# Converting weight pieces in pairs, fetching the first piece first, and a lag of one block in batch 0

## The chip, the cores and the metric

The kernel runs on one core of a Trainium2 chip. The metric is device time in microseconds, the median of several executions. The core has five engines with instruction queues of their own: PE (matmuls), DVE and ACT (elementwise), POOL, and SP, which here issues every DMA. Each engine takes its instructions in the order in which they were built, and waits on semaphores for the others.

## The reference, cut to what matters

For 8 batches of 8 heads, 576 rows of 64 columns, 32 packed rows per head attend to the whole sequence, and then the sequence attends to the 32 packed results. The attention output is reshaped to 4608 tokens of 512 columns and goes through a two-layer network with a Mish activation. The weights are of type float64, as numpy makes them.

```python
p_packed = sm_attn(p, k, v)                      # softmax(scale * p k^T) v
out = sm_attn(q, p_packed, p_packed)
x = attn_out.transpose(0, 2, 1, 3).reshape(B * S, H * D)
h = x @ w_in                                     # 512 x 2048
g = h * np.tanh(sp)                              # sp = log1p(exp(h)), Mish
return g @ w_out                                 # 2048 x 512
```

## The kernel before

**Stages.** An opening computes the attention of batch 0, written out step by step. After it a loop runs over `t`, one step for each batch `b` and block `f` of 128 of the 2048 hidden columns (16 blocks per batch, `NF`). In each step PE does the up product of block `f` in two halves of 288 tokens (`Group.up`, L618 to L634) and the down product of an earlier block in four parts of 128 tokens (`down`, L660; part c is "down c"). ACT applies Mish to each up half and writes `g`. The earlier block is `LAG` = 2 steps back. The attention of batch b + 1 is a generator (`Later.attention`) that is advanced some two or three times in a step, so that it lies between these products.

**Up without the values matrix.** The up product uses `packed_w` (L570): for each chunk of 512 hidden columns (4 blocks) the packed values of the batch are multiplied into w_in once, 16 matmuls into two PSUM tiles `ps_w`; ACT writes the high part `wp_hi`, DVE the low part `wp_lo`. In batch 0, chunk c + 1 is packed in the last block of chunk c (f = 3, 7, 11), between down 2 and the second up half. `ps_w` shares its two PSUM buffers (`ps_a`) with the scores and values of the attention.

**Weights.** w_in and w_out arrive as 32 pieces of 512 KB of 64-bit words (`Weight`: chunk c, row block m; `WeightOut`: block f). A piece is fetched by one DMA into one of `STB` = 10 stage buffers (`fetch`); ACT makes two passes over its words, one into the destination and one into a buffer `wround`, of which there are 3 (`words`); DVE joins them in four steps, each of which works on the result of the one before (`join`, L550 to L559). The last step frees `wround`; the third is the last that reads the stage buffer. In batch 0 the down product uses w_out as converted; later batches use a high and a low half, made by `split_wo` from step 14 on.

**What sets the order.** In the opening PE and SP stand in the order of the code, and DVE and ACT are put in order by a scheduler when the program is built. From the end of the opening to step 16 all of them stand in the order of the code, except that a few of the first of these rows are placed among the last of the opening. Behind step 16 the scheduler orders SP, DVE and ACT again. `upto` (L731) and `join_next` (L739) decide which piece is fetched, gets its words and is joined: after the four pieces of chunk 0, w_in and w_out pieces alternate, and each step joins two, one after up 0 and one after up 1, with words one piece ahead. A stage buffer is refilled when the piece ten places ahead of it has been joined.

Of the kernel before, what the change touches and what calls it, by code (L numbers as in the profile page):

```python
# [16 lines left out]
LAG = 2  # L17
# [3 lines left out]
STB = 10  # L21
# [13 lines left out]
def body(  # L35
# [22 lines left out]
    NF = DF // P  # L58
# [52 lines left out]
    def load_heads(src, b, g, tag):  # L111
        ts = []
        for h0 in (4 * g, 4 * g + 2):
            t = early.tile([R, 2, NI, 2 * D], F32, name=tag, tag="kvq", bufs=KVB)
            nc.sync.dma_start(
                out=t, in_=src[b, h0:h0 + 2].rearrange("h (p i x) d -> p h i (x d)", i=NI, x=2)
            )
            ts.append(t)
        return ts
# [411 lines left out]
    class Weight:  # L531
# [18 lines left out]
        def join(self):  # L550
            dst, bits = self.dst, self.dst.bitcast(I32)
            nc.vector.tensor_scalar(
                out=dst, in0=dst, scalar1=F64_HIGH, scalar2=-F64_HIGH, op0=ALU.min, op1=ALU.max
            )
            nc.vector.tensor_scalar(out=bits, in0=bits, scalar1=3, scalar2=None, op0=ALU.logical_shift_left)
            nc.vector.scalar_tensor_tensor(
                out=bits, in0=self.high, scalar=-0x80000000, in1=bits, op0=ALU.bitwise_and, op1=ALU.bitwise_or
            )
            nc.vector.tensor_tensor(out=bits, in0=bits, in1=self.r, op=ALU.add)  # L559

    class WeightOut(Weight):
# [146 lines left out]
    def advance(gen):  # L708
        flush()
        next(gen, None)  # L710
# [11 lines left out]
    n_groups = B * NF  # L722

    pieces = [Weight(0, m) for m in range(4)]
    for f in range(NF):
        if f < 12:
            pieces.append(Weight(1 + f // 4, f % 4))
        pieces.append(WeightOut(f))
    pieces_done = {"fetch": 0, "words": 0, "join": 0}

    def upto(step, n):  # L731
        while pieces_done[step] < min(n, len(pieces)):
            k = pieces_done[step]
            getattr(pieces[k], step)()
            pieces_done[step] += 1
            if step == "join":
                upto("fetch", k + 1 + STB)

    def join_next(n):  # L739
        for _ in range(n):  # L740
            k = pieces_done["join"]
            upto("words", k + 1)
            upto("join", k + 1)
            upto("words", k + 2)

    with tc.manual_schedule(engines={mybir.EngineType.PE}):
        for _ in range(8):
# [1 line left out]
        first = batches[0]  # L749
        by_hand = ExitStack()  # L750
        by_hand.enter_context(tc.manual_schedule(engines={mybir.EngineType.SP}))
        first.k_t = [load_heads(k, 0, 0, "k_t")]
        first.load_p()
        upto("fetch", 1)
        first.k_t.append(load_heads(k, 0, 1, "k_t"))
        first.v_t = [load_heads(v, 0, 0, "v_t")]
        first.q_t = [load_heads(q, 0, 0, "q_t")]
        upto("fetch", 2)
        first.v_t.append(load_heads(v, 0, 1, "v_t"))
        first.q_t.append(load_heads(q, 0, 1, "q_t"))  # L760
        upto("fetch", STB)
        first.start(ps_a)
        score = [first.score_now(g) for g in range(2)]
        for _ in range(3):
            next(score[0])
        upto("words", 1)
        next(score[0], None)
        upto("join", 1)
        next(score[1])
        next(score[1])  # L770
        together(first.turn_weights(0, ps_acc, ("ACT", "ACT")))
        next(score[1])
        next(score[1], None)
# [2 lines left out]
        together(first.turn_values(0, ps_a))  # L776
        together(first.turn_weights(1, ps_acc, ("ACT", "ACT")))
        together(first.match(0, ps_acc))
        upto("words", 2)
        first.peak(slice(0, 1))  # L780
        first.rise(slice(0, 1))
        upto("join", 2)
        together(first.values(1, ps_a))
        together(first.turn(1, ps_acc, ("ACT", "ACT", "ACT")))
        together(first.turn_values(1, ps_a))
        together(first.match(1, ps_acc))
        upto("words", 3)
        first.peak(slice(1, 2))
        first.rise(slice(1, 2))
        first.weigh(slice(0, 1))  # L790
        upto("words", 4)
        upto("join", 4)
        wps = {(0, 0): packed_w(0, 0)}
        first.weigh(slice(1, 2))
        by_hand.enter_context(tc.manual_schedule(engines={mybir.EngineType.DVE, mybir.EngineType.Activation}))
        upto("words", 5)
        groups = []
        gen = iter(())
        g_rest = None
        for t in range(n_groups + LAG):  # L800
            b, f = divmod(t, NF)
            grp = None
            if t < n_groups:
                if f == 0:
                    if b % 2 == 0:
                        g_rest = ([], [])
                if f == (1 if b else ATT0) and b + 1 < B:
                    gen = batches[b + 1].attention()
                if t == LOAD0:
                    opening.close()  # L810
                    kv.append(ctx.enter_context(tc.tile_pool(name="kv", bufs=2, side="left", reuse_waits="tile")))
                    for _ in range(KQB):
                        load_next()
                grp = Group(b, f, wps[b, f // 4], g_rest)
                grp.tiles()
            groups.append(grp)
            dn = groups[t - LAG] if t >= LAG else None
            joins = 2 if t < 14 else 0
            if t == NF:
                by_hand.close()  # L820
            if t == SPLIT0:
                stage.close()
                late.append(ctx.enter_context(tc.tile_pool(name="late", bufs=1, side="right", reuse_waits="tile")))
            if 0 <= t - SPLIT0 < NF:
                split_wo(t - SPLIT0)
            if dn:
                down(dn, 0)
            if grp:
                grp.up(0)
            chunk = b == 0 and f % 4 == 3 and f < NF - 1  # L830
            if not chunk:
                advance(gen)
            join_next(joins - joins // 2)
            if dn:
                down(dn, 1)
                down(dn, 2)
            if chunk:
                flush()
                wps[0, f // 4 + 1] = packed_w(0, f // 4 + 1)
            else:  # L840
                advance(gen)
            if grp:
                grp.up(1)
                grp.halves()
            join_next(joins // 2)
            if dn and dn.b % 2 == 1 and dn.f % 4 == 2:
                rest["g"] = split(dn.g_rest[0][dn.f // 4], dn.g_rest[1][dn.f // 4])
            if dn:
                down(dn, 3)
            if grp and f % 4 == 2 and (b or f == NF - 2):  # L850
                nb, nch = divmod(b * (NF // 4) + f // 4 + 1, NF // 4)
                if nb < B:
                    flush()
                    if nb > b:
                        finish(gen)
                    wps[nb, nch] = packed_w(nb, nch)
            elif b == 0 and not chunk:
                advance(gen)
            if dn and dn.b % 2 == 1 and dn.f % 4 == 3:
                flush()  # L860
                down_rest(dn)
# [26 lines left out]
```

## Time and profile before

| | us |
|---|---|
| median of 3 runs (778.96 to 779.28) | 779.27 |
| the profiled execution, whole | 777.98 |
| its span, first to last instruction | 776.2 |
| PE busy | 740.1 (95%) |
| DVE busy | 440.8 (57%) |
| ACT busy | 297.3 (38%) |

In the page's 40 slices of 19.4 us, PE stands at 6, 7, 7, 7, 8, 9 and 6 tenths in the first seven and at 9 after that. All 32 weight pieces arrive in the first six slices, in which the mean busy share of the DMA engines is 8 to 9 tenths or more. Times below are in microseconds from the start of the span. A row of the order of time gives start, duration, engine, line, operation, output and inputs, count, and in brackets the idle time before it and what ended it. Durations of neighbours on one engine can overlap, so what a row costs its engine is read from start to start. A matmul in 32 bits shows as two records, so four records of `acc` are two downs.

### The profile page before, as it was taken

The numbers are of one execution on the slowest core, as the hardware profiler recorded it, in microseconds if no ns is written. First come the engines' busy times: TensorE is split into PE (matmuls) and PEld (weight loads), VectorE is DVE, ScalarE is ACT, GpSimd is POOL, SyncE is SP. The second block draws the span as 40 slices with busy tenths as digits, with TensorE's granted clock in tenths as the row PEclk, the third lists the DMA queues.
The fourth block names the chain that finished last, engine by engine and source line by source line (L and its number), as shares of the span: only waits on it lengthen the run. The fifth ranks groups of instructions, "written<-read, shape, count | busy, mean of one in ns | idle before, by whom it ended". The sixth has DMA issues, their size and how long they took to land.

```text
span 776.2 us, 12461 instructions
## 1 busy us (share of the span) xinstructions
PE 740.1 (95%) x5044; PEld 565.9 (73%) x5044; DVE 440.8 (57%) x788; ACT 297.3 (38%) x685; POOL 0.7 (0%) x6
## 2 busy tenths in 40 slices
PE   6777896999999999999999999999999999999997
PEld 4453553568788787878788787878788787888886
DVE  4888898964663636554663636554673636432332
ACT  3563654824242334224342244224242244322221
POOL 0000000000000000000000000000000000000000
PEclk9998998999999999999999999999999999999999
DMA  9999980032510534032510434032400200010002
GB/s 248 338 194 275 223 197 0 1 86 41 98 23 1 119 58 84 1 85 38 103 21 1 113 61 86 1 85 32 92 1 1 69 2 1 1 55 1 0 1 69
DMA packets 184825, 56.39 MB, mean 73 GB/s; under 512 B 173760, under 2 KB 176064, under 8 KB 184768
## 3 DMA queue, kind: packets, MB, share of 16 engines
q1 hardware_dynamic: 184768, 55.59, 30.8%
q8 instruction: 40, 0.66, 0.4%
q14 instruction: 17, 0.14, 0.1%
HBM read 46.14 MB, written 9.44 MB: 72 GB/s over the span
## 4 chain that ended last, share of the span: by engine, by line
PE 85%; DVE 6%; DMA 5%; SPq 2%; issue 1%; ACT 0%; DVEq 0%
PE ps_h L627 25%; PE acc L646 15%; PE acc L648 13%; PE acc L647 13%; PE ps_w L577 5%; PE acc L666 3%; DMA w_st<-in_moe_w_in_dram 3%; PE ps_s L396 2%; PE ps_rest L647 2%; PE ps_rest L648 2%; PE ps_rest L646 2%; SPq L341 2%; DMA w_st<-in_moe_w_out_dram 1%; PE ps_pp L451 1%; DVE xT L386 1%
## 5 line engine op out<-in xcount | busy, mean ns | idle before, releaser
L630 ACT ACTIVATE g<-ps_h 128x288 f32<-128x288 f32 (+1 forms) x256 | 97.6, 384 | 322.7 <-PE ps_h L627 293.3
L646 PE MATMUL acc<-wo_hi,g_hi 128*128 128x512 f32 x448 | 183.9, 410 | 0.0
L648 PE MATMUL acc<-wo_hi,g_lo 128*128 128x512 f32 x448 | 176.4, 394 | 0.0
L647 PE MATMUL acc<-wo_lo,g_hi 128*128 128x512 f32 x448 | 176.2, 393 | 0.0
L627 PE MATMUL ps_h<-aT_hi,wp_hi 128*128 128x288 f32 x512 | 165.2, 323 | 4.7 <-ACT aT_hi L297 4.7
L627 PE MATMUL ps_h<-aT_lo,wp_hi 128*128 128x288 f32 x512 | 152.8, 298 | 1.4 <-DVE aT_lo L300 1.4
L627 PE MATMUL ps_h<-aT_hi,wp_lo 128*128 128x288 f32 x512 | 152.0, 297 | 0.0
L641 DVE CAST g_hi<-g 128x512 fp32r<-128x512 f32 x112 | 47.6, 425 | 169.8 <-ACT g L630 169.6
L627 PEld LDWEIGHTS ps_h<-aT_hi,wp_hi 128*128 128x128 f32 x512 | 97.7, 191 | 27.1 <-issue 7.5
L646 PEld LDWEIGHTS acc<-wo_hi,g_hi 128*128 128x128 f32 x448 | 84.0, 187 | 43.4 <-issue 28.4
L627 PEld LDWEIGHTS ps_h<-aT_lo,wp_hi 128*128 128x128 f32 x512 | 97.8, 191 | 17.0 <-issue 6.0
L648 PEld LDWEIGHTS acc<-wo_hi,g_lo 128*128 128x128 f32 x448 | 84.0, 188 | 19.7
L627 PEld LDWEIGHTS ps_h<-aT_hi,wp_lo 128*128 128x128 f32 x512 | 97.7, 191 | 0.0
L647 PEld LDWEIGHTS acc<-wo_lo,g_hi 128*128 128x128 f32 x448 | 84.3, 188 | 9.0 <-issue 0.2
L642 DVE TENSOR_TENSOR g_lo<-g,g_hi 128x512 fp32r<-128x512 f32 x112 | 77.3, 690 | 6.3 <-DVE g_hi L641 0.5
L666 PE MATMUL acc<-wo,g 128*128 128x512 f32 x128 | 63.2, 609 | 0.0
L577 PE MATMUL ps_w<-wi,ppT 64*32 64x512 f32 x512 | 41.8, 634 | 15.1 <-DVE wi L559 7.1
L589 DVE TENSOR_TENSOR wp_lo<-ps_w,wp_hi 128x512 fp32r<-128x512 f32 x64 | 41.3, 683 | 24.8 <-ACT wp_hi L588 24.8
L588 ACT CAST wp_hi<-ps_w 128x512 fp32r<-128x512 f32 x64 | 34.4, 590 | 50.4 <-PE ps_w L577 50.4
L666 PEld LDWEIGHTS acc<-wo,g 128*128 128x128 f32 x128 | 22.7, 196 | 15.4 <-issue 13.8
L577 PEld LDWEIGHTS ps_w<-wi,ppT 64*32 64x32 f32 x512 | 7.6, 108 | 31.4 <-issue 17.1
L632 ACT ACTIVATE g_rest<-ps_h 128x64 f32<-128x64 f32 x128 | 28.1, 220 | 0.0
(107 smaller groups left out, 688.8 us busy)
## 6 DMA issues: line engine op xcount, KB each, us to landing
w_st<-in_moe_w_in_dram SPq DMA_DIRECT2D x16, 512.0 KB, 7.8
w_st<-in_moe_w_out_dram SPq DMA_DIRECT2D x16, 512.0 KB, 5.7
k_n<-in_k_dram SPq DMA_DIRECT2D x56, 144.0 KB, 3.1
q_n<-in_q_dram SPq DMA_DIRECT2D x56, 144.0 KB, 3.2
v_n<-in_v_dram SPq DMA_DIRECT2D x56, 128.0 KB, 2.8
out_dram<-o SPq DMA_DIRECT2D x28, 256.0 KB, 2.0
k_t<-in_k_dram SPq DMA_DIRECT2D x4, 288.0 KB, 5.0
v_t<-in_v_dram SPq DMA_DIRECT2D x4, 288.0 KB, 8.6
```

Source lines behind the costliest of these rows:

```text
L577: nc.tensor.matmul(out=ps[g][h * NP:(h + 1) * NP, :], lhsT=ppTb[row:row + D, g, h * NP:(h + 1) * NP], rhs=wi[c][g][row:row + D, h // 2, :] ...
L588: nc.scalar.copy(out=hi, in_=ps[g])
L589: nc.vector.tensor_tensor(out=lo, in0=ps[g], in1=hi.bitcast(F32), op=ALU.subtract)
L627: nc.tensor.matmul(out=ps, lhsT=w[:, fs], rhs=a[:, g, cs], start=(n == 0), stop=(n == 5))
L630: nc.scalar.activation(out=self.act[:, hf * HALF:hf * HALF + m], in_=ps[:, :m], func=AF.Mish)
L632: nc.scalar.activation(out=self.g_rest[self.b % 2][self.f // 4][:, self.f % 4, :], in_=ps[:, m:], func=AF.Mish)
L641: nc.vector.tensor_copy(out=hi, in_=self.act)
L642: nc.vector.tensor_tensor(out=lo, in0=self.act, in1=hi.bitcast(F32), op=ALU.subtract)
L646: nc.tensor.matmul(out=acc, lhsT=hi[:, cs], rhs=wh, start=start, stop=False)
L647: nc.tensor.matmul(out=acc, lhsT=hi[:, cs], rhs=wl, start=False, stop=False)
L648: nc.tensor.matmul(out=acc, lhsT=lo[:, cs], rhs=wh, start=False, stop=stop)
L666: nc.tensor.matmul(out=accs[c], lhsT=grp.act[:, cs], rhs=wo[f], start=f == 0, stop=f == NF - 1)
```

## The change

The diff, without the functions that it replaces:

```diff
             nc.vector.tensor_scalar(
                 out=dst, in0=dst, scalar1=F64_HIGH, scalar2=-F64_HIGH, op0=ALU.min, op1=ALU.max
             )
+            yield
             nc.vector.tensor_scalar(out=bits, in0=bits, scalar1=3, scalar2=None, op0=ALU.logical_shift_left)
+            yield
...
     pieces = [Weight(0, m) for m in range(4)]
-    for f in range(NF):
-        if f < 12:
-            pieces.append(Weight(1 + f // 4, f % 4))
-        pieces.append(WeightOut(f))
...
+    pieces += [WeightOut(0), Weight(1, 0), Weight(1, 1), WeightOut(1), Weight(1, 2), Weight(1, 3)]
+    pieces += [WeightOut(2), WeightOut(3)]
+    for c in (2, 3):
+        for e in range(2):
+            pieces += [Weight(c, 2 * e), Weight(c, 2 * e + 1), WeightOut(4 * c - 4 + 2 * e), WeightOut(4 * c - 3 + 2 * e)]
+    pieces += [WeightOut(i) for i in range(12, NF)]
...
+    def join(n):
+        words(n)
+        together(*[x.join() for x in pieces[done["join"]:n]])
+        done["join"] = max(done["join"], min(n, len(pieces)))
+        fetch(n + STB)
...
+        fetch(1)
         first.k_t = [load_heads(k, 0, 0, "k_t")]
         first.load_p()
-        upto("fetch", 1)
         first.k_t.append(load_heads(k, 0, 1, "k_t"))
+        fetch(2)
...
-            dn = groups[t - LAG] if t >= LAG else None
-            joins = 2 if t < 14 else 0
+            lag = 1 if t <= NF else LAG
+            dn = groups[t - lag] if t >= lag and t != NF + 1 else None
...
-            join_next(joins - joins // 2)
+            if t <= 12:
+                words(2 * t + 8)
+                join(2 * t + 8)
+                words(2 * t + 10)
             if dn:
                 down(dn, 1)
-                down(dn, 2)
             if chunk:
                 flush()
                 wps[0, f // 4 + 1] = packed_w(0, f // 4 + 1)
-            else:
+            if dn:
+                down(dn, 2)
+            if not chunk:
                 advance(gen)
...
-            join_next(joins // 2)
```

In words: `join` is now a generator that stops after each step, and two pieces are joined with their steps in turn (first piece step 1, second piece step 1, first piece step 2, and so on). In the loop one pair is joined per step, after up 0, and the words of the next pair follow it. The pieces are in another order: each chunk of w_in is now joined two steps or more before it is packed, and w_out blocks come one step before their down product. In the opening `join(2)`, `join(4)` and `join(6)` stand where single pieces stood, and the first weight DMA is the first DMA of all. In batch 0 the down product lags one step instead of two (step 17 has none, so that later batches lag two again), and in the last block of a chunk the packed weights come before down 2 instead of behind it.

Three places show what the change does to the queues. First, ACT in the opening, behind the exponentials of the first scores' second half: `wi0`, `wi1` are w_in of chunk 0 and 1, `wo32` is w_out, `qT` and `a1T` are copies that the attention of batch 0 needs. Before:

```order
L547 ACTIVATE wi0_1_92<-w_st_145 128x512
L548 ACTIVATE wround_426<-w_st_145 128x512
L547 ACTIVATE wi0_1_92<-w_st_147 128x512
L548 ACTIVATE wround_442<-w_st_147 128x512
L133 COPY qT_305<-ps_kq_306 128x384
L133 COPY qT_305<-ps_kq_312 128x384
L547 ACTIVATE wi1_0_93<-w_st_149 128x512
L133 COPY qT_305<-ps_kq_318 128x384
L548 ACTIVATE wround_487<-w_st_149 128x512
L133 COPY a1T_327<-ps_a1_328 96x384
L133 COPY a1T_327<-ps_a1_333 96x384
```

Now:

```order
L547 ACTIVATE wi0_1_92<-w_st_147 128x512
L548 ACTIVATE wround_429<-w_st_147 128x512
L547 ACTIVATE wo32_151<-w_st_149 128x512
L548 ACTIVATE wround_484<-w_st_149 128x512
L133 COPY qT_315<-ps_kq_316 128x384
L547 ACTIVATE wi1_0_93<-w_st_152 128x512
L548 ACTIVATE wround_487<-w_st_152 128x512
L133 COPY qT_315<-ps_kq_322 128x384
L133 COPY qT_315<-ps_kq_328 128x384
L547 ACTIVATE wi1_0_93<-w_st_154 128x512
L548 ACTIVATE wround_506<-w_st_154 128x512
L133 COPY a1T_337<-ps_a1_338 96x384
```

Counted in the order of fetching, the words of the fourth to the seventh piece now stand between these exponentials and the a1T copies; before, those of the third to the fifth did. On DVE eight pieces instead of five are joined ahead of the first `wp_lo`.

Second, DVE in step 10, where the attention of batch 1 takes its row maxima (`mx2`) and subtracts them. Before (third w_in piece of chunk 3, then w_out of block 10):

```order
L272 TENSOR_REDUCE mx2_1161<-a2_1090 128x36
L273 TENSOR_TENSOR a2_1090<-a2_1090,mx2_1161 128x1152
L552 TENSOR_SCALAR wi3_1_98<-wi3_1_98 128x512
L555 TENSOR_SCALAR wi3_1_98<-wi3_1_98 128x512
L556 SCALAR_TENSOR_TENSOR wi3_1_98<-w_st_829,wi3_1_98 128x512
L559 ISA wi3_1_98<-wi3_1_98,wround_1145 128x1024
L552 TENSOR_SCALAR wo32_861<-wo32_861 128x512
L555 TENSOR_SCALAR wo32_861<-wo32_861 128x512
L556 SCALAR_TENSOR_TENSOR wo32_861<-w_st_859,wo32_861 128x512
L559 ISA wo32_861<-wo32_861,wround_1168 128x1024
```

Now (w_out of blocks 10 and 11):

```order
L272 TENSOR_REDUCE mx2_1182<-a2_1111 128x36
L273 TENSOR_TENSOR a2_1111<-a2_1111,mx2_1182 128x1152
L552 TENSOR_SCALAR wo32_860<-wo32_860 128x512
L552 TENSOR_SCALAR wo32_863<-wo32_863 128x512
L556 TENSOR_SCALAR wo32_860<-wo32_860 128x512
L556 TENSOR_SCALAR wo32_863<-wo32_863 128x512
L558 SCALAR_TENSOR_TENSOR wo32_860<-w_st_858,wo32_860 128x512
L558 SCALAR_TENSOR_TENSOR wo32_863<-w_st_861,wo32_863 128x512
L562 ISA wo32_860<-wo32_860,wround_1142 128x1024
L562 ISA wo32_863<-wo32_863,wround_1145 128x1024
```

The two pieces behind the subtraction are a pair in turn, and both are of w_out: the piece of w_in that stood here now comes one step earlier, and the last one of chunk 3, which stood in step 11, two steps earlier.

Third, ACT in the same step, around the exponential of the attention (L279), which needs a table load before and after it. `g` is Mish of an up half. Before:

```order
L547 ACTIVATE wi3_1_98<-w_st_829 128x512
L548 ACTIVATE wround_1145<-w_st_829 128x512
L630 ACTIVATE g_1151<-ps_h_1153 128x288
L547 ACTIVATE wo32_861<-w_st_859 128x512
L548 ACTIVATE wround_1168<-w_st_859 128x512
L279 ACT_TABLE_LOAD
L279 ACTIVATE a2_1090<-a2_1090 128x1152
L630 ACT_TABLE_LOAD
L630 ACTIVATE g_1151<-ps_h_1174 128x224
```

Now:

```order
L633 ACTIVATE g_1172<-ps_h_1174 128x288
L547 ACTIVATE wo32_925<-w_st_923 128x512
L548 ACTIVATE wround_1193<-w_st_923 128x512
L547 ACTIVATE wo32_928<-w_st_926 128x512
L548 ACTIVATE wround_1196<-w_st_926 128x512
L279 ACT_TABLE_LOAD
L279 ACTIVATE a2_1111<-a2_1111 128x1152
L633 ACT_TABLE_LOAD
L633 ACTIVATE g_1172<-ps_h_1202 128x224
```

Words of two pieces, instead of one, stand between the first half's `g` and the exponential, and they are those of the pair that DVE joins one step later (`wo32_925` and `wo32_928`, w_out of blocks 12 and 13).

More of the change, by code (lines that the diff above doesn't have):

```diff
@@ L558, in join @@
             )
+            yield
             nc.vector.tensor_tensor(out=bits, in0=bits, in1=self.r, op=ALU.add)
@@ L724, in body, with fetch, words @@
     pieces = [Weight(0, m) for m in range(4)]
-    for f in range(NF):
-        if f < 12:
-            pieces.append(Weight(1 + f // 4, f % 4))
-        pieces.append(WeightOut(f))
[L729 to L744, printed above, removed]
+    pieces += [WeightOut(0), Weight(1, 0), Weight(1, 1), WeightOut(1), Weight(1, 2), Weight(1, 3)]
[4 more added lines that the diff above has]
+    pieces += [WeightOut(i) for i in range(12, NF)]
+    done = {"fetch": 0, "words": 0, "join": 0}
+    def fetch(n):
+        for x in pieces[done["fetch"]:n]:
+            x.fetch()
+        done["fetch"] = max(done["fetch"], min(n, len(pieces)))
+    def words(n):
+        for x in pieces[done["words"]:n]:
+            x.words()
+        done["words"] = max(done["words"], min(n, len(pieces)))
+    def join(n):
[3 more added lines that the diff above has]
+        fetch(n + STB)
     with tc.manual_schedule(engines={mybir.EngineType.PE}):
@@ L751, in body @@
         by_hand.enter_context(tc.manual_schedule(engines={mybir.EngineType.SP}))
+        fetch(1)
         first.k_t = [load_heads(k, 0, 0, "k_t")]
         first.load_p()
-        upto("fetch", 1)
         first.k_t.append(load_heads(k, 0, 1, "k_t"))
+        fetch(2)
         first.v_t = [load_heads(v, 0, 0, "v_t")]
         first.q_t = [load_heads(q, 0, 0, "q_t")]
-        upto("fetch", 2)
+        fetch(3)
         first.v_t.append(load_heads(v, 0, 1, "v_t"))
         first.q_t.append(load_heads(q, 0, 1, "q_t"))
-        upto("fetch", STB)
+        fetch(STB)
         first.start(ps_a)
@@ L765, in body @@
             next(score[0])
-        upto("words", 1)
         next(score[0], None)
-        upto("join", 1)
         next(score[1])
         next(score[1])
+        join(2)
         together(first.turn_weights(0, ps_acc, ("ACT", "ACT")))
@@ L778, in body @@
         together(first.match(0, ps_acc))
-        upto("words", 2)
         first.peak(slice(0, 1))
         first.rise(slice(0, 1))
-        upto("join", 2)
         together(first.values(1, ps_a))
@@ L786, in body @@
         together(first.match(1, ps_acc))
-        upto("words", 3)
+        join(4)
         first.peak(slice(1, 2))
@@ L790, in body @@
         first.weigh(slice(0, 1))
-        upto("words", 4)
-        upto("join", 4)
         wps = {(0, 0): packed_w(0, 0)}
         first.weigh(slice(1, 2))
+        join(6)
         by_hand.enter_context(tc.manual_schedule(engines={mybir.EngineType.DVE, mybir.EngineType.Activation}))
-        upto("words", 5)
+        words(8)
         groups = []
```

## The prediction

> **What bounds the kernel now.** I read the busy rows in forty slices first: PE is full from about 136 us to the end, so only the first sixth can move. The view of who waited for whom, for PE up to 170 us, then names the waits.
>
> ```profile
> PE ps_w L577 <- DVE wi L559: 7.1, 1, 7.1
> PE ps_w L577 <- DVE a L416: 5.6, 1, 5.6
> PE ps_w L577 <- DVE pp L242: 2.4, 1, 2.4
> ```
>
> Columns: total us, times, longest. The three largest all stand before packed weights (`ps_w`) of chunk 3, 1 and 2, and all end on DVE: 15.1 us. Two windows of 5 us, one within the wait of 5.6 and one behind that of 2.4 (length, busy time of PE, its weight loads, DVE, ACT and POOL, granted clock, DMA share, GB/s):
>
> ```profile
> 60.00:65.00 5.00, 0.88 (x9) 0.43 (x16) 4.13 (x10) 0.00 (x0) 0.00 (x0) 0.56 1.04 278
> 95.00:100.00 5.00, 5.00 (x28) 3.31 (x32) 4.34 (x9) 2.58 (x7) 0.00 (x0) 0.68 0.99 209
> ```
>
> So DVE works (4.13 of 5) while PE waits (0.88), and around each wait the granted clock falls (0.56, 0.68). The chain that ended last prices this (start, us, what):
>
> ```profile
> 64.12 2.38 PE ps_w L577 x16
> 66.50 1.46 PE ps_h L627 x6
> ...
> 93.70 1.09 PE ps_w L577 x14
> 94.79 1.74 PE ps_h L627 x6
> 96.53 2.59 PE acc L666 x4
> ...
> 127.75 1.92 PE ps_w L577 x6
> 129.68 1.74 PE ps_h L627 x6
> 131.41 2.22 PE acc L666 x4
> 133.63 0.80 PE ps_h L627 x6
> 134.43 1.72 PE acc L666 x4
> ...
> 147.85 1.02 PE ps_w L577 x16
> ```
>
> At full clock an up half is 0.80, two downs 1.72 (0.86 each), packed weights 1.02. Excess after the first wait: 1.36 + 0.66 = 2.0; after the second 0.2 + 0.94 + 0.87 = 2.0; after the third (6 of 16 should be 0.38) 1.54 + 0.94 + 0.50 = 3.0. Waits and half clock together: 22 us, the most that can be won here.
>
> **Steps in turn.** One piece alone, then independent DVE steps, from the order of time:
>
> ```profile
> 60.05 0.42 DVE L552 TENSOR_SCALAR wi<-wi 128x512 f32<-128x512 f32 x1
> ...
> 60.97 0.69 DVE L556 SCALAR_TENSOR_TENSOR wi<-w_st,wi 128x512 int32<-128x512 int32 x1
> 61.80 0.69 DVE L559 CUSTOM_DVE_ANT_0 wi<-wi,wround 128x1024 uint16<-128x1024 uint16 x1
> 62.41 0.82 DVE L412 TENSOR_REDUCE mx<-ps_s 128x1 f32<-128x288 f32 x2
> ```
>
> ```profile
> 24.96 0.69 DVE L559 CUSTOM_DVE_ANT_0 wi<-wi,wround 128x1024 uint16<-128x1024 uint16 x1
> 25.57 0.42 DVE L555 TENSOR_SCALAR wi<-wi 128x512 int32<-128x512 int32 x1
> 25.90 0.28 DVE L250 COPY ppT<-ps_ppT 128x128 f32<-128x128 f32 x1
> 26.10 0.68 DVE L556 SCALAR_TENSOR_TENSOR wi<-w_st,wi 128x512 int32<-128x512 int32 x1
> 26.70 0.42 DVE L552 TENSOR_SCALAR wi<-wi 128x512 f32<-128x512 f32 x1
> ```
>
> A piece whose steps wait for each other costs 2.36 (60.05 to 62.41): its third step holds the fourth up for 0.83 (60.97 to 61.80). Where the next step is independent it starts 0.61, 0.33 and 0.60 after (24.96, 25.57 and 26.10), before the former has ended. A pair in turn is therefore 2 x (0.33 + 0.33 + 0.60 + 0.61) = 3.75 instead of 4.72: 0.95 won per pair. Bounds: nothing, or 0.95; I take the rows of independent steps. Here a rule speaks against the change: the Trainium skill, "VectorE: DVE Perf Modes", section "The DRAIN you can't avoid", says that the next DVE operation does not start until the pipe is empty and that leaving out semaphores saves nothing, though it adds that an operation which is not held starts earlier. Taken by its first statement, order wins nothing and the first rival below is the outcome. This trace disagrees with that statement: 25.57 with 0.42 of duration is followed at 25.90.
>
> **The opening.** Now 8 pieces instead of 5 are converted on DVE before the first packed low half, and ACT takes their words in landing order between its copies.
>
> ```profile
> 6.04 0.66 PE L182 MATMUL ps_p<-ident,p_t 128*128 128x128 f32 x2 [1.20 <-DMA p_t<-in_p_dram]
> 8.36 0.66 ACT L547 ACTIVATE wi<-w_st 128x512 f32<-128x512 f32 x1 [0.50 <-DMA w_st<-in_moe_w_in_dram]
> 16.82 0.66 ACT L547 ACTIVATE wi<-w_st 128x512 f32<-128x512 f32 x1 [2.56 <-DMA w_st<-in_moe_w_in_dram]
> 17.39 0.66 ACT L548 ACTIVATE wround<-w_st 128x512 int32<-128x512 uint32 x1
> 25.94 0.67 ACT L547 ACTIVATE wi<-w_st 128x512 f32<-128x512 f32 x1 [0.40 <-DMA w_st<-in_moe_w_in_dram]
> 27.46 0.85 ACT L133 COPY a1T<-ps_a 96x384 f32<-96x384 f32 x2
> 42.02 0.67 ACT L297 CAST aT_hi<-at 128x576 fp32r<-128x576 f32 x1 [3.62 <-DVE at L294]
> ```
>
> The first piece now goes ahead of k and p on the one SP queue, and their bytes land in the other order: p at about 8.3 instead of 6.0, so PE starts 2.3 later. The fifth piece still lands at 25.9, since the bytes ahead of it are the same. ACT then does, in order: its words 2 x 0.57 (16.82 to 17.39), one qT copy 0.43, words 1.14, two copies 0.85, words 1.14, the two a1T copies 0.85: they end at 31.5, not 28.3: +3.2. DVE then meets three steps of the seventh and eighth piece (0.60 + 0.61 + 0.61) among the transposes of the second half's scores, and a sum that stood before them: +2.2. So aT_hi at 42.02 becomes about 47.4: **+5.4**. Bounds: +2.3 (p alone), and 2.3 + 3 x 2.36 = +9.4 (three pieces wholly in the way).
>
> **Chunk by chunk**, since DVE sets the pace.
>
> Chunk 1: from the opening to packed weights both kernels convert six pieces. The first pair wins nothing (ACT's words for it, 4 x 0.57, are as slow); two pairs win 1.9. So 64.12 + 5.4 - 1.9 = 67.6. PE came there at 64.12 - 5.6 = 58.5; with 5.4, and three more downs (2.6) by lag 1, it comes at 66.5 at the latest, less the small waits for DVE that the later start covers (1 to 2): its wait falls from 5.6 to 1 to 3. I keep 2.0 for the half clock, as after 5.6 and 2.4. Hence +3.5 in time with 2.6 us of downs done ahead.
>
> Chunk 2: eight pieces as four pairs win 3.8 on DVE. But the scores of half 1 now come after one more down. DVE is ready for them 1.5 + 0.6 + 1.3 (packed weights, first wp_hi, wp_lo) + 3.75 = 7.1 behind the start of packed weights; PE has them after 1.02 + 5 x 0.86 + 2 x 0.80 + 2.0 of half clock = 8.9, so DVE waits 1.8. DVE arrives at 93.70 + 3.5 - 3.8 + 1.8 = 95.2. PE: a chunk (16 downs, 8 up halves, packed weights, the part of attention) took 93.70 to 119.58 below, less 2.0 of half clock, 23.9: 67.6 + 23.9 + 2.0, and 1 to 2 more since an a1T copy on ACT stands behind two pieces' words: 94.5 to 95.5. So 95.4 and hardly a wait.
>
> ```profile
> 95.48 1.29 DVE L589 TENSOR_TENSOR wp_lo<-ps_w,wp_hi 128x512 fp32r<-128x512 f32 x2 [1.83 <-ACT wp_hi L588]
> 114.49 1.28 ACT L279 ACT_TABLE_LOAD   x1
> 115.20 1.36 DVE L273 TENSOR_TENSOR a<-a,mx 128x1152 f32<-128x1152 f32 x1
> 116.59 1.17 ACT L279 ACTIVATE a<-a 128x1152 f32<-128x1152 f32 x1 [0.82 <-DVE a L273]
> 119.58 1.07 PE L577 MATMUL ps_w<-wi,ppT 64*32 64x512 f32 x10
> 121.19 1.35 DVE L285 TENSOR_REDUCE sm<-a 128x36 f32<-128x1152 f32 x1
> 125.30 0.38 DVE L552 TENSOR_SCALAR wi<-wi 128x512 f32<-128x512 f32 x1
> 129.72 1.07 ACT L588 CAST wp_hi<-ps_w 128x512 fp32r<-128x512 f32 x2 [7.64 <-PE ps_w L577]
> ```
>
> Chunk 3: the wait of 7.1 for `wi` goes, because its last pair is done two blocks ahead. New ones come. From wp_lo (95.48) to the end of the subtraction (116.56) DVE took 21.1 with five pieces; now two pairs, 4.3 less, and some 1.5 of waiting for PE's match (between nothing and the 1.8 of chunk 2). wp_lo starts at 95.4 + 1.8 as before and 0.3 for the words now ahead of wp_hi, 97.5: 97.5 + 16.8 + 1.5 = 115.8. Only then comes the pair of w_out 10 and 11, whose first is whole after 4 x 0.33 + 2 x 0.60 + 0.69 = 3.2, at 119.0. With lag 1, down of block 10 needs it at 95.4 + 23.9 - 2.5 = 116.8: a wait of 2.2. The words of w_out 13 need a `wround` buffer (there are three) that the same step frees; the exponential stands behind them on ACT: 119.0 + 0.57 + 1.28 + 1.17 = 122.0, where before it began at 116.59. DVE's sums wait for it: +4.1 (121.19 to 125.30) = 126.1; then the pair 12/13, whose first, whole 3.2 later at 129.3, frees the buffer for the words ahead of wp_hi: 129.3 + 0.57 + 0.6 = 130.5, the 0.6 being half of 1.07 and a start. The first up half of block 12 starts at about 131.2, with 0.5 in it of waiting for the low halves; before, 133.63. That is 2.4 earlier with four more downs done (3.4): 5.8, less 0.5, less 2.0 of half clock: **-3.3**. The half clock after the wait at 116.8 costs nothing more, as PE waits again at 131 anyhow.
>
> **What I cost at nothing.** Packed weights one down earlier: PE swaps two neighbours; cover for wp_hi and wp_lo (0.6 + 1.3) grows from 2.5 to 3.4; without cover it costs the 1.9. Block 17 has no down: its matmuls move, and the split of g still has three downs and three up halves (5 us) to hide behind. Later batches have the same matmuls, and PE is full there. DMA: behind 25.94 the view of waits has no wait of ACT or DVE for a weight's landing, so landing order binds only in the opening.
>
> The span goes from 776.2 to 772.9, the profiled time from 777.98 to 774.7, and the median from 779.27 to **776.0**.
>
> **Rivals.** (1) Steps in turn win nothing, by a DVE that empties between operations. The ten pairs behind the opening's then cost 0.95 each: +9.5, so +6.2, 785.5. The overlapping rows speak against it: 0.06. (The section of the Trainium skill named above, by its first statement, would give this.) (2) The opening costs more: ACT's queue is held by the landing of pieces. It decides from +8.7, where the gain is used up; at the upper bound +9.4 and one more half-clock window (2.0) it gives 782. For it: 2.56 of ACT idle at 16.82 for a landing; against it: the bytes are the same. 0.14. (3) No new waits: DVE stays ahead of PE. Then 15.1 + 7.0 go, 5.4 stays: -16.7, 762.6. For it: 22 us of PE waits; against it: in-order `wround` and the exponential, and a DVE already busy for 4.1 to 4.3 of 5. 0.12 for that and anything beyond -8. (4) Gain and cost cancel within 0.2%, about 1.6 us, which is what a measurement of this kernel can tell from no change: 0.17.
>
> **How the numbers follow.** The forecast, -1.6 to -8 us, has 0.51. Faster: 0.51 + 0.12 = 0.63; same 0.17; slower 0.06 + 0.14 = 0.20. The opening's bounds alone give -6.4 to +0.7; half a clock window each way widens that to -8 and +2.7. The range reaches a little into rivals 2 and 3: 768.5 to 782.5, leaving 0.09 below and 0.09 above.
>
> **What would show it.** Right: aT_hi of half 1 near 47; pairs of 3.75 on DVE; PE's waits for `ps_w` small or gone but for chunk 1 (1 to 3); new PE waits for `wo` before down of block 10 and for wp_hi at block 12; exponential near 121 to 122. Wrong: pairs of 4.7 (rival 1); aT_hi past 51 (rival 2); no wait on PE past 70 (rival 3); or a wait in batch 1, which I cost at nothing.

## The result, and the profile after

The changed kernel takes 771.06 us (median of 4 runs, 769.48 to 772.07) against 779.27 beside it (4 runs, 778.96 to 780.49, one more than in the table of the kernel before): a ratio of 0.989, with a 95% interval of 0.9868 to 0.9911. It was timed again in a later comparison: 771.58 against 778.00, 0.9921 (0.9908 to 0.9934). So it is faster by about 1%, and the gain is clear of the noise in both comparisons: 8.2 in the first, 6.4 in the second. The profiled execution went from a span of 776.2 to 769.6, 6.6 less.

Waits of PE in the first 170 us of the changed kernel, the ones that matter below (line waited for, sum in us, times, longest):

```profile
PE ps_h L630 <- ACT aT_hi L297: 7.2, 2, 6.5
PE ps_h L630 <- ACT wp_hi L591: 3.3, 1, 3.3
...
PE ps_p L182 <- DMA p_t<-in_p_dram: 3.1, 1, 3.1
PE acc L669 <- DVE wo L562: 2.7, 1, 2.7
PE ps_w L580 <- DVE a L416: 2.2, 1, 2.2
...
PE acc L669 <- ACT g L633: 1.2, 2, 1.0
```

The three waits at packed weights (5.6, 2.4 and 7.1 before) have become one of 2.2. Two new ones stand before and at chunk 3, at the down of block 10 for `wo` and at the up half of block 12 for wp_hi, and the opening's wait for aT_hi has grown from 4.7 to 7.2. PE in order of time (start, us, engine, line, tiles, count, wait before it and its releaser):

```profile
65.67 1.51 PE L580 MATMUL ps_w<-wi,ppT 64*32 64x512 f32 x16 [2.17 <-DVE a L416]
...
91.28 1.70 PE L580 MATMUL ps_w<-wi,ppT 64*32 64x512 f32 x16
...
116.42 1.10 PE L669 MATMUL acc<-wo,g 128*128 128x512 f32 x2 [2.71 <-DVE wo L562]
...
122.98 1.88 PE L669 MATMUL acc<-wo,g 128*128 128x512 f32 x4
...
128.12 0.40 PE L630 MATMUL ps_h<-aT_hi,wp_hi 128*128 128x288 f32 x1 [3.26 <-ACT wp_hi L591]
...
129.85 3.22 PE L669 MATMUL acc<-wo,g 128*128 128x512 f32 x4
```

Two downs (four records) take 1.88 at full clock (122.98) and 3.22 at 129.85: half clock follows the wait of 3.26 (granted clock 0.50 from 130 to 132), and none follows the 2.17 and the 2.71 (1.00 from 66 to 72 and from 116 to 122). But for 0.2 at 128.85, PE does not wait again behind 128.12. On ACT and DVE of the changed kernel, the places that hold up the two new waits and chunk 3 (first block), and DVE from the opening on (second block):

```profile
116.36 0.67 ACT L548 ACTIVATE wround<-w_st 128x512 int32<-128x512 uint32 x1 [3.89 <-DVE wo L562]
117.04 1.28 ACT L279 ACT_TABLE_LOAD   x1
118.34 1.16 ACT L279 ACTIVATE a<-a 128x1152 f32<-128x1152 f32 x1
...
126.94 0.67 ACT L548 ACTIVATE wround<-w_st 128x512 int32<-128x512 uint32 x1 [3.15 <-DVE wo L562]
127.51 1.05 ACT L591 CAST wp_hi<-ps_w 128x512 fp32r<-128x512 f32 x2
```

```profile
46.38 0.76 DVE L300 TENSOR_TENSOR aT_lo<-at,aT_hi 128x576 fp32r<-128x576 f32 x1 [0.74 <-ACT aT_hi L297]
...
60.25 0.72 DVE L552 TENSOR_SCALAR wi<-wi 128x512 f32<-128x512 f32 x2
60.88 0.75 DVE L556 TENSOR_SCALAR wi<-wi 128x512 int32<-128x512 int32 x2
...
63.96 0.81 DVE L412 TENSOR_REDUCE mx<-ps_s 128x1 f32<-128x288 f32 x2
...
93.72 1.29 DVE L592 TENSOR_TENSOR wp_lo<-ps_w,wp_hi 128x512 fp32r<-128x512 f32 x2 [1.87 <-ACT wp_hi L591]
...
100.24 0.49 DVE L463 COPY ppT<-ps_ppT 128x128 f32<-128x128 f32 x2 [1.23 <-PE ps_ppT L462]
102.66 0.85 DVE L472 STREAM_TRANSPOSE a<-ps_s 128x288 f32<-128x288 f32 x2 [1.93 <-PE ps_s L396]
...
119.53 1.35 DVE L285 TENSOR_REDUCE sm<-a 128x36 f32<-128x1152 f32 x1 [2.66 <-ACT a L279]
```

A pair takes 3.71 (60.25 to 63.96). The chain of chunk 3 can be read row by row: the step at L562 makes w_out 10 whole and frees a `wround` (116.3), the blocked words run, then the exponential that stands behind them, then DVE's sum (after 2.66 idle), then the next pair, then the next blocked words (126.94), then wp_hi, then PE (128.12).

### The profile page after: what moved, and what is told of

Its sections match the earlier page's. It is cut to its first block, busy times and chain, and to the rows that moved or that the text cites. A ratio compares the mean times of both kernels' runs of the same rounds, so it can differ in the third digit from the quotient of the medians.

```text
span 769.6 us, 12465 instructions
## 1 busy us (share of the span) xinstructions
PE 735.9 (96%) x5044; PEld 563.7 (73%) x5044; DVE 433.7 (56%) x788; ACT 298.3 (39%) x685; POOL 0.7 (0%) x6
## 4 chain that ended last, share of the span: by engine, by line
PE 87%; DMA 4%; DVE 3%; SPq 2%; ACT 2%; issue 1%; DVEq 0%; ACTq 0%
PE ps_h L630 25%; PE acc L649 15%; PE acc L651 14%; PE acc L650 13%; PE ps_w L580 4%; PE acc L669 4%; DMA w_st<-in_moe_w_in_dram 3%; PE ps_s L396 2%; PE ps_rest L650 2%; PE ps_rest L651 2%; PE ps_rest L649 2%; SPq L341 2%; PE ps_pp L451 1%; PE ps_a L438 1%; DMA p_t<-in_p_dram 1%
## 5 line engine op out<-in xcount | busy, mean ns | idle before, releaser
L669 PE MATMUL acc<-wo,g 128*128 128x512 f32 x128 | 64.9, 617 | 3.9 <-DVE wo L562 2.7
L580 PE MATMUL ps_w<-wi,ppT 64*32 64x512 f32 x512 | 38.4, 612 | 2.2 <-DVE a L416 2.2
L651 PE MATMUL ps_rest<-wo_hi,r_lo 128*128 128x512 f32 x64 | 25.1, 392 | 0.0
```

The source lines that it names most:

```text
L580: nc.tensor.matmul(out=ps[g][h * NP:(h + 1) * NP, :], lhsT=ppTb[row:row + D, g, h * NP:(h + 1) * NP], rhs=wi[c][g][row:row + D, h // 2, :] ...
L651: nc.tensor.matmul(out=acc, lhsT=lo[:, cs], rhs=wh, start=False, stop=stop)
L669: nc.tensor.matmul(out=accs[c], lhsT=grp.act[:, cs], rhs=wo[f], start=f == 0, stop=f == NF - 1)
```

## The experiments

All were timed beside the kernel before; the ratio is to it. The spans are those of one profiled execution each. The second to the fifth row come from one comparison, the last two from another, the remaining four from a third; medians of different comparisons are set side by side by their ratios alone.

| run | span, us | median, us | ratio, 95% interval |
|---|---|---|---|
| changed kernel, again | 769.4 | 771.58 | 0.9921 (0.9908 to 0.9934) |
| steps not in turn | 777.6 | 779.80 | 1.0020 (1.0010 to 1.0029) |
| four `wround` | 763.6 | 766.36 | 0.9841 (0.9829 to 0.9854) |
| first piece behind k and p | 772.4 | 774.40 | 0.9940 (0.9924 to 0.9955) |
| lag 2 | 773.0 | 777.16 | 0.9977 (0.9965 to 0.9988) |
| packed weights behind down 2 | 766.1 | 768.43 | 0.9882 (0.9870 to 0.9895) |
| four `wround`, w_out 10 first | 768.3 | 767.82 | 0.9886 (0.9870 to 0.9903) |
| six pieces in the opening | 778.6 | 779.53 | 1.0011 (0.9994 to 1.0028) |
| four `wround`, packed late | 763.6 | 765.11 | 0.9822 (0.9808 to 0.9837) |
| the same, w_out 10 first, 12 behind | 765.0 | 766.26 | 0.9839 (0.9825 to 0.9853) |

### What two executions of one program differ by

> The changed kernel itself, beside the others on one chip, for the comparison and for what differs between two executions of the same program. Every theory expects 769 to 772 us of time less 1.5 to 2.2 for the span; a difference between its two profiles bounds what may be read from a difference between two kernels in one profile.

The span was 769.4, and packed weights of chunk 1 began at 65.39 instead of 65.67. In all kernels here with this opening and steps in turn, chunk 1 begins between 64.4 and 66.1, and the words of the third piece on ACT between 16.6 and 18.0: that much varies between single executions of kernels that are the same up to there, so what lies behind chunk 1 is compared by its distance from the start of these packed weights. PE of this second execution:

```profile
91.01 1.69 PE L580 MATMUL ps_w<-wi,ppT 64*32 64x512 f32 x16
...
116.14 2.04 PE L669 MATMUL acc<-wo,g 128*128 128x512 f32 x2 [2.71 <-DVE wo L562]
...
127.85 0.40 PE L630 MATMUL ps_h<-aT_hi,wp_hi 128*128 128x288 f32 x1 [1.49 <-ACT wp_hi L591]
...
129.58 3.32 PE L669 MATMUL acc<-wo,g 128*128 128x512 f32 x4
```

After the same wait of 2.71 one down takes 2.04 here and took 1.10 in the first execution: half clock in one and not in the other. Here half clock also follows a wait of 1.49 (3.32 for two downs at 129.58). Yet block 12 begins at the same distance behind chunk 1 (62.46 and 62.45): half clock ahead of a wait that ACT and DVE end only shortens that wait, from 3.26 to 1.49.

### Steps not in turn

```diff
-        together(*[x.join() for x in pieces[done["join"]:n]])
+        for x in pieces[done["join"]:n]:
+            together(x.join())
```

> The changed kernel with the steps of the pieces of one join no longer in turn: one piece's four DVE steps, then the next one's. Everything else as changed. Theory (steps in turn are what makes DVE shorter): a pair costs 4.7 us instead of 3.71, about 0.95 more for each of the ten pairs behind the opening; DVE sets the pace of chunks 1 and 3 and nearly of chunk 2, so the span of 769.6 grows by 4 to 9.5, to about 775 (ratio to the kernel before 0.995 to 1.003). Packed weights of chunk 1 then start near 67.6 (65.67 with the change) and w_out 10 is whole near 121. Rival A (order on DVE wins nothing since the pipe empties anyway): pair cost and span unchanged, 769 to 770.5. Rival B (it does shorten DVE, but the gain comes from the order of pieces and the lag): pairs 4.7, span 770 to 772.

DVE of this run, a pair ahead of chunk 1's scores:

```profile
61.55 0.38 DVE L552 TENSOR_SCALAR wi<-wi 128x512 f32<-128x512 f32 x1
...
66.22 0.81 DVE L412 TENSOR_REDUCE mx<-ps_s 128x1 f32<-128x288 f32 x2
```

61.55 to 66.22 is 4.67, against 3.71: 0.96 a pair. The span is 8.0 longer, packed weights of chunk 1 begin at 67.92, and w_out 10 is waited for until 123.27. The theory holds, near the upper end of its range; both rivals fall. Without turns the change is worth nothing (1.0020): the order of the steps carries more than the whole gain. The old wait of 7.1 at the packed weights of chunk 3 does not come back in this run, which keeps the new order of the pieces and the lag of one; that order was not tried by itself.

### Four buffers for wround

```diff
-            self.r = stg.tile([P, FC], I32, name="wround", bufs=3)
+            self.r = stg.tile([P, FC], I32, name="wround", bufs=4)
```

> The changed kernel with four buffers for wround instead of three; nothing else. Theory (the two new waits of PE at blocks 10 to 12 come from words on ACT that wait for a buffer, with the exponential and the wp_hi copies behind them): ACT's waits of 3.89 and 3.15 for wo go, the exponential starts near 113 instead of 118.3, DVE's wait of 2.66 at 119.5 goes, PE's wait of 3.26 for wp_hi falls under 1, and with it the half clock behind 128; the wait of 2.7 for w_out 10 stays, since DVE's order ahead of it is the same. Span 764 to 767, about 765.5 (ratio 0.982 to 0.987). Rival (DVE's order alone holds these waits, or PE's time comes back in a later wait): within 1 of 769.6.

ACT, then PE of this run:

```profile
111.43 0.65 ACT L548 ACTIVATE wround<-w_st 128x512 int32<-128x512 uint32 x1
112.10 1.28 ACT L279 ACT_TABLE_LOAD   x1
113.39 1.16 ACT L279 ACTIVATE a<-a 128x1152 f32<-128x1152 f32 x1
...
121.63 1.07 ACT L591 CAST wp_hi<-ps_w 128x512 fp32r<-128x512 f32 x2
```

```profile
115.41 1.57 PE L669 MATMUL acc<-wo,g 128*128 128x512 f32 x2 [2.71 <-DVE wo L562]
```

The words no longer wait, the exponential begins 5 earlier, DVE's sum (L285) runs at 115.78 without idle ahead of it, and there is no wait of PE behind 115.41. PE's and DVE's orders are those of the changed kernel, row for row, and on ACT two neighbours swap. The span is 6.0 shorter, of which 1.0 is this execution's earlier chunk 1 (64.67). So the buffer was worth 5, where the theory said 4, and it is shown that the second new wait and its half clock hung on `wround`. The wait of 2.71 for w_out 10 stays to the digit: that one is DVE's order.

### First piece behind k and p

```diff
-        fetch(1)
         first.k_t = [load_heads(k, 0, 0, "k_t")]
         first.load_p()
+        fetch(1)
```

> The changed kernel with the first piece loaded behind the first k and p again. Theory (the late p makes a part of the opening's 3.7 us by itself, the whole chain behind it being moved): p's first transpose near 6.0 instead of 7.9, aT_hi of half 1 about 1.9 earlier, packed weights of chunk 1 near 63.8, and the span 1.5 to 2 shorter, near 767.9 (ratio 0.986 to 0.988). Rival (the conversions on ACT and DVE set the opening, and the first piece comes later by as much): aT_hi within 0.5 of 46.4, span within 0.5 of 769.6 or up to 1 longer.

ACT and DVE of this run:

```profile
19.10 0.66 ACT L547 ACTIVATE wi<-w_st 128x512 f32<-128x512 f32 x1 [3.90 <-DMA w_st<-in_moe_w_in_dram]
...
24.59 0.67 ACT L547 ACTIVATE wi<-w_st 128x512 f32<-128x512 f32 x1 [2.58 <-DMA w_st<-in_moe_w_in_dram]
...
27.50 0.66 ACT L547 ACTIVATE wo<-w_st 128x512 f32<-128x512 f32 x1 [1.32 <-DMA w_st<-in_moe_w_out_dram]
```

```profile
48.90 0.76 DVE L300 TENSOR_TENSOR aT_lo<-at,aT_hi 128x576 fp32r<-128x576 f32 x1 [0.74 <-ACT aT_hi L297]
```

Both guesses were wrong. p's transpose does begin at 5.81 instead of 7.93, yet the low half of aT comes 2.5 later than in the changed kernel, and the span is 2.8 longer. ACT waits in order for every piece, with the copies for PE behind the words: 3.90, 2.58 and 1.32 here. In the changed kernel the same pieces' words, from the third on:

```profile
18.03 0.66 ACT L547 ACTIVATE wi<-w_st 128x512 f32<-128x512 f32 x1 [1.48 <-DMA w_st<-in_moe_w_in_dram]
...
23.28 0.67 ACT L547 ACTIVATE wi<-w_st 128x512 f32<-128x512 f32 x1 [0.46 <-DMA w_st<-in_moe_w_in_dram]
...
24.55 0.68 ACT L547 ACTIVATE wo<-w_st 128x512 f32<-128x512 f32 x1
```

The fifth piece there has landed before ACT comes to it; with the old order ACT waits for it until 27.50. Why the pieces land later here is open. In the first 30 us the DMA engines moved 8.92 MB in the changed kernel and 8.54 here, but the kernel before, whose first transfer is one of k too, also moved 8.92, and the executions of the other kernels with the changed opening and turns moved 8.77 to 9.32.

By the profiles, loading the first piece ahead is a gain of its own, although p comes later by it: the low half of aT (48.90) and chunk 1 (68.19) come later here than in every execution with the changed opening and turns (45.09 to 46.80, and 64.4 to 66.1). By the times alone it is not shown, since the intervals of the ratios (0.9924 to 0.9955, and 0.9908 to 0.9934 for the changed kernel again) overlap.

### Lag of two blocks

```diff
-            lag = 1 if t <= NF else LAG
-            dn = groups[t - lag] if t >= lag and t != NF + 1 else None
+            dn = groups[t - LAG] if t >= LAG else None
```

> The changed kernel with a lag of two blocks throughout, as before the change. Theory (where PE waits for DVE or ACT at the packed weights, it has four downs fewer behind it and owes them at the end of batch 0): the wait of 2.7 for w_out 10 goes, but the wait at the wp_hi of block 12 grows to 6 to 8 and four downs (3.4) are left over: span +2 to +4, 771.6 to 773.6 (ratio 0.992 to 0.997). Rival (lag only moves waits from one place to another): within 1 of 769.6. Second rival (the wait for w_out 10 delays DVE's transposes by way of PE, so without it DVE is earlier too): span 1 to 2 shorter.

Waits of PE in this run's first 170 us, those behind the opening that changed:

```profile
PE ps_w L580 <- DVE a L416: 5.0, 1, 5.0
PE ps_h L630 <- ACT g_rest L635: 3.3, 2, 3.1
...
PE ps_h L630 <- ACT wp_hi L591: 1.6, 1, 1.6
```

The span is 3.4 longer, or 4.6 behind chunk 1, which began at 64.42 here; by the ratios (0.9977 against 0.9921) the time is about 4.4 longer. Four downs are 3.4; the packed weights behind the longer wait take 2.38 instead of 1.51, at half clock again. The theory holds, its price by the ratio just above its range (0.992 to 0.997). Its detail does not: the wait at block 12 did not grow to 6 to 8, but came in two parts, one for a PSUM buffer whose Mish stands behind the exponential, one for wp_hi. Chunk 1 waits 5.0 instead of 2.2.

### Packed weights behind down 2

```diff
             if dn:
                 down(dn, 1)
+                down(dn, 2)
             if chunk:
                 flush()
                 wps[0, f // 4 + 1] = packed_w(0, f // 4 + 1)
-            if dn:
-                down(dn, 2)
```

> The changed kernel with the packed weights of chunks 1 to 3 back behind the third of the block's four downs. Theory (the move swaps two neighbours on PE, and costs or wins nothing where PE waits for DVE anyway): PE's wait for a at chunk 1 falls from 2.2 to about 1.3, as one more down lies ahead, and the cover of wp_hi and wp_lo falls from 3.4 to 2.5; span within 1 of 769.6, ratio 0.988 to 0.991. Rival (the earlier start of the packed weights is what shortens the wait for wp_hi at blocks 4, 8 and 12): span 1.5 to 2.7 longer.

PE of this run:

```profile
90.64 1.09 PE L580 MATMUL ps_w<-wi,ppT 64*32 64x512 f32 x16
...
114.33 1.34 PE L669 MATMUL acc<-wo,g 128*128 128x512 f32 x2 [2.72 <-DVE wo L562]
...
126.04 0.40 PE L630 MATMUL ps_h<-aT_hi,wp_hi 128*128 128x288 f32 x1 [2.04 <-ACT wp_hi L591]
...
127.60 1.88 PE L669 MATMUL acc<-wo,g 128*128 128x512 f32 x4
```

A miss, although the ratio lies just within the range that was written down: the span is 3.3 shorter than in the second execution of the changed kernel, and the intervals of the two ratios, of one comparison, are apart. Of the 3.3, 0.4 is the earlier chunk 1 (65.03 against 65.39). At chunk 2 the packed weights begin at the same distance behind chunk 1 (25.6), but with one more down done, and they take 1.09 instead of 1.69. (In the changed kernel fourteen of their sixteen weight loads wait 0.48 there for DVE's `pp`.) From there w_out 10 is whole 1.45 sooner; DVE's wait for PE's transposes (`ps_ppT`) falls from 1.2 to 0.4. The last 1.44 is the half clock that does not follow block 12's wait here (1.88 against 3.32 for two downs). So moving the packed weights ahead of the third down costs about 1.4 by itself, and up to 2.9 with the half clock, which differs between executions of one program and is read here from one of each.

### Four buffers, and w_out 10 ahead on DVE

Besides `bufs=4` for `wround` as above:

```diff
+            if t == 10:
+                join(28)
             if not chunk:
                 advance(gen)
```

> The changed kernel with four buffers for wround and with the steps for w_out 10 and 11 put on DVE ahead of batch 1's maximum and subtraction (L386, L272, L273) instead of behind them; nothing else. Theory (the last wait of PE in batch 0, 2.7 for w_out 10, comes from DVE's order alone): w_out 10 is whole near 112 instead of 115.4, PE's wait before down of block 10 falls under 0.5, the half clock behind it (1.5 us) goes too; the exponential starts some 3.7 later, at about 116 to 117, which PE does not meet before block 12; span 759.5 to 761.5, where four buffers alone gave 763.6 (ratio 0.978 to 0.981). Rival (the later exponential holds ACT, and PE waits for ps_h or g behind it instead): span 763 to 765.

PE, then DVE of this run:

```profile
119.54 1.12 PE L669 MATMUL acc<-wo,g 128*128 128x512 f32 x2 [2.26 <-ACT g L633]
```

```profile
125.68 1.28 DVE L592 TENSOR_TENSOR wp_lo<-ps_w,wp_hi 128x512 fp32r<-128x512 f32 x2
```

The wait for w_out 10 is gone, but the kernel is slower than with four buffers alone (0.9886 against 0.9841). The exponential begins at 116.66, and PE waits 2.26 for a g whose Mish stands behind it on ACT, then 2.7 for wp_lo, which comes 1.3 later behind chunk 1 than with four buffers alone (123.60 with chunk 1 at 64.67, here 125.68 with 65.42). The rival was right in kind. Its price was too low: 763 to 765 was written down, the profiled execution has 768.3, and the spans of the five executions go from 765.5 to 768.3.

### Six pieces in the opening

```diff
-        words(8)
         groups = []
...
-            if t <= 12:
+            if 1 <= t <= 12:
                 words(2 * t + 8)
```

> The changed kernel with six pieces converted in the opening instead of eight: the seventh and eighth are done with the ninth and tenth in block 1. Theory (the two further pieces are the rest of the opening's 3.7, 1.9 being the late p, but DVE needs the time for them before the packed weights of chunk 1 either way): aT_hi of half 1 near 43.5 instead of 45.7 (its low half at 44.2 instead of 46.38), packed weights of chunk 1 at 65 to 67, span within 1.5 of 769.6. Rival (the opening's delay carries through to the end): packed weights of chunk 1 at 63.5, span 767 to 768.

DVE, PE and ACT of this run:

```profile
43.69 0.76 DVE L300 TENSOR_TENSOR aT_lo<-at,aT_hi 128x576 fp32r<-128x576 f32 x1 [0.74 <-ACT aT_hi L297]
```

```profile
59.83 2.05 PE L669 MATMUL acc<-wo,g 128*128 128x512 f32 x2 [6.53 <-DVE wo L562]
```

```profile
59.18 0.67 ACT L548 ACTIVATE wround<-w_st 128x512 int32<-128x512 uint32 x1 [4.90 <-DVE wi L562]
```

The first half holds: aT's low half comes 2.7 earlier (43.69 against 46.38), so most of the opening's 3.66 is the seventh and eighth piece. The second half is a miss, by 9 us of span, or about 7 by the ratios (1.0011 against 0.9921). In block 1 four pieces now go in turn, and the last step of the first of them comes only when the third steps of all four are done, so that w_out 1, the second of them, is late (whole at 59.7), PE waits 6.53 for it, and ACT, with three `wround` for four pieces, waits 4.90. Not all of the 6.53 is the turn: w_out 1 is also converted a block later, and ACT takes its words only at 51.39. One after the other at 2.36 a piece from 50.95 on, w_out 1 would be whole at 55.7, an estimate from the first steps of this run (50.95 on DVE) and the row of a dependent piece in the prediction; so some 4 of the 6.53 are put down to the turn, which was not tried apart. The turn shortens the sum of a join and delays its first pieces, the more the more pieces there are.

### The two that win, together

> The changed kernel with four buffers for wround and with the packed weights of chunks 1 to 3 back behind the third down. Theory (the two edits win in different places: the buffer on ACT and DVE behind 112, the third down at the packed weights of chunks 1 and 2, where DVE sets the start and one down was owed): the gains add for the most part, 0.9 to 1.5 beyond four buffers alone, span 761.5 to 763 (ratio 0.980 to 0.983). Rival (both win the same half clock behind block 10, so that with one of them the other is worth nothing): span 763.5 to 764.5.

Both edits stand above: `bufs=4` for `wround`, and the packed weights behind down 2. Where chunk 1 begins in this run:

```profile
66.10 1.51 PE L580 MATMUL ps_w<-wi,ppT 64*32 64x512 f32 x16 [1.21 <-DVE a L416]
```

The span is 763.6 with chunk 1 at 66.10, 1.4 later than in the run with four buffers alone, and the median is 765.11, ratio 0.9822 against 0.9841. Behind chunk 1 it wins 1.4 on that run, which is what the third down was worth before the half clock. The profiled span lies in the rival's range (763.5 to 764.5); for the theory speak this distance, the ratio (0.980 to 0.983 was written down) and that three of the five executions have spans below that range (761.2 to 763.0). The intervals of the two ratios overlap, so by the times alone it is likely, not shown, that it beats four buffers. It has the lowest ratio here, 1.8% below the kernel before and 1% below the change (0.9921).

### w_out 10 ahead, and 12 and 13 behind wp_lo

Beside the edits of the last run, w_out 10 and 11 are joined ahead as above, and in block 11 nothing is joined:

```diff
+            if t == 12:
+                join(30)
-            if t <= 12:
+            if t <= 12 and t != 11:
```

> As the run above, and in addition w_out 10 and 11 ahead of batch 1's maximum and subtraction on DVE, and w_out 12 and 13 behind the low halves of the packed weights of chunk 3 instead of ahead of them, with the words of w_out 14 and 15 behind wp_hi on ACT. Theory (putting w_out 10 ahead failed before because the later exponential pushed w_out 12 and 13, and wp_lo behind them, back by 2; with those behind wp_lo it wins): wait for w_out 10 gone, wp_lo of chunk 3 near 121, span 758.5 to 761 (ratio 0.975 to 0.980). Rival (PE then waits for g behind the late exponential, 2.3 as before, and pays its half clock there): span 761.5 to 764.

PE of this run:

```profile
117.66 2.07 PE L669 MATMUL acc<-wo,g 128*128 128x512 f32 x2 [3.28 <-ACT g L633]
```

The rival holds in kind, with the profiled 765.0 a little above its range of 761.5 to 764 (762.9 to 765.0 in four executions). wp_lo came at 122.33, near the 121 expected, but PE waits 3.28 for a g whose Mish stands on ACT behind the exponential, which began at 114.78, and pays its half clock there. The wait at block 10 changes its owner and does not go. Whether another place of the exponential on ACT would free it was not tried.

## Why the prediction was right

The forecast was 776.0, 3.3 below before; it came out at 771.06. Direction and mechanism were right, two terms were too dear, and one that was put at nothing was not nothing. The band that had the highest chance (-1.6 to -8) holds the 6.4 of the second comparison and just misses the 8.2 of the first, which falls into the band beyond -8, with 0.12. By places in the profile:

| place | forecast | measured | off by |
|---|---|---|---|
| low half of aT, later than 42.72 by (aT_hi: 45.68 against 42.02) | 5.4 | 3.66 | -1.7 |
| packed weights, chunk 1 | 67.6 | 65.67 | -1.9 |
| packed weights, chunk 2 | 95.4 | 91.28 | -4.1 |
| down of block 10 | 119.0 | 116.42 | -2.6 |
| up half of block 12 | 131.2 | 128.12 | -3.1 |
| span | 772.9 | 769.6 | -3.3 |

- **Steps in turn**, 3.75 a pair: measured 3.71, and 4.67 when undone. Right, and it is the gain. By its first statement, the Trainium skill, "VectorE: DVE Perf Modes", section "The DRAIN you can't avoid", would have made the turn worthless; the run without turns speaks against that (8.0 of span), and with its addition on operations that are not held.
- **The opening**, +5.4: mis-sized, measured +3.66. The step that failed was "the fifth piece still lands at 25.9, since the bytes ahead of it are the same": its words began at 24.55 and no longer waited for a landing. In the run with the old load order the third to the fifth piece came 1 to 3 us later. The two further pieces cost 2.7, within what was summed for them.
- **Chunk 1**, a wait of 1 to 3: 2.17, right. The **half clock of 2.0** charged after it did not come in any execution with a wait of 2.0 to 2.2 there, nor after 3.28 in the run without turns (granted clock 1.00 from 67.9 to 74). This is the second mis-sized term: with the 1.9 of chunk 1 it makes 3.9 of the 4.1 at chunk 2.
- **Chunk 3**: w_out 10 was to be waited for 2.2 and took 2.71; the exponential was to begin at 120.8 (the 122.0 of the working is its end, although it is set beside a beginning there), and began at 118.34, 1.9 behind w_out 10 as forecast; block 12 followed 11.7 behind it (forecast 12.2). Right by its own steps, and the run with four `wround` shows the cause. From wp_lo (93.72) to w_out 10 it took 22.7, where 21.5 was forecast: DVE waited 1.23 and 1.93 there for PE's transposes and match, 2.3 more than the 0.84 before, where 1.5 was forecast with a bound of 1.8. This gave back 1.2 of the 4.1. The run with the packed weights behind down 2 shows where some of it came from, next point.
- **Packed weights one down earlier**, costed at nothing: wrong by 1.4 to 2.9. The cover of wp_hi and wp_lo was looked at. What was not seen is that where DVE sets the start of the packed weights (chunk 1, and most of their loads at chunk 2), a down moved behind them is owed afterwards.
- **Lag of one block**, four downs of 3.4 won: undone, it costs 3.4 of span and 4.6 behind chunk 1, 4.4 by the ratios.

The 3.3 by which the span undercut the forecast is so made up: 1.9 at chunk 1, nearly all from the opening; 2.0 of half clock behind it; 1.2 given back to DVE's waits for the match; 0.5 won between blocks 10 and 12; and 0.1 of smaller ones. That errors of 3.9 one way and 1.2 the other partly cancel is luck. Rival 1 falls by the run without turns, rival 2 by aT at 46, rival 3 by the two new waits, and rival 4 by the intervals of both ratios, which end below 0.998. One reading of the view of waits was off, without a part in the sum: the three waits named are not the three largest, since aT_hi (4.7 in two) and `ps_pp` (3.2) stand above the 2.4; they are the largest behind the opening.

## What to carry to other kernels

Where an engine runs dependent short steps, interleave the steps of two independent pieces: it added no instruction here and carried the gain. With four pieces, look first at who waits for the early ones. A buffer count is part of an in-order queue: one buffer short, and an instruction that nobody waits for holds up those behind it that others do (here an exponential, 5 us for 2 KB a partition). Read moves at a place that another engine sets by what is owed behind them, not by the cover ahead of them.

## What was not expected of the hardware

- Half clock after a wait is not set by its length alone: after 2.71 one execution of the same program ran at full clock (one down in 1.10), another at half (2.04); half clock also followed a wait of 1.49 in that other, and full clock a wait of 3.28 in the run without turns. This agrees with the Trainium skill, "TensorE: Matmul & The Clock Gate", section "Part 1: The HAM clock gate (the "warmup" mystery)", which has the activity watched in a free-running window, so that the same kernel shows different numbers of slow matmuls. A fixed 2.0 per wait, as in the prediction, is too simple.
- The granted clock and the durations can disagree. In the run with four `wround` the clock stands at 1.00 in the window from 45 to 50 us, while single matmuls of 288 columns take 0.44 and start 0.24 apart there, 0.29 and 0.13 some us further on:

```profile
46.84 0.44 PE L630 MATMUL ps_h<-aT_hi,wp_hi 128*128 128x288 f32 x1
47.08 0.44 PE L630 MATMUL ps_h<-aT_lo,wp_hi 128*128 128x288 f32 x1
```

  In the other runs with this opening the window shows 0.50 with the same durations, and the kernel before shows 1.00 with starts 0.24 apart in the same window. So the clock is read together with the durations.
- With the first piece behind k and p, ACT began on the third to the fifth piece at 19.10, 24.59 and 27.50, each time behind a wait for the landing, against 18.03, 23.28 and 24.55 in the changed kernel, in one execution. The third differs by up to 1.4 between executions with the changed opening, so the 2.95 at the fifth is the firmer sign. Why stays open.
